# Moving three pieces of VectorE's order, and half of the last stores to a second queue, in a transform-and-ELU kernel

## The chip, the cores and the metric

The kernel runs on one core of a Trainium2 chip. The metric is the device time of one execution in microseconds (us). Every experiment was run several times on one chip together with runs of the kernel before, and is compared with those alone. One execution of each kernel was taken with the hardware profiler; quoted profile lines are from it. Where medians are given they are of all executions of the row.

## The reference

```python
batch, seq, dim = 8, 3008, 256          # x: float32
X = np.fft.fft(np.fft.fft(x, axis=1), axis=2).real
h = X.reshape(24064, 256) @ w_in        # w_in: 256 x 2048
g = np.where(h > 0, h, np.exp(np.minimum(h, 0)) - 1)
out = g @ w_out                         # w_out: 2048 x 256
```

## The kernel before

The transform over the channels is folded into the weights: W1 becomes a cosine part Wc and a sine part Ws. What is left of the transform runs over the sequence, as matrix products with constants (MC); it fills rings from which the tiles read: Rr (real part), Ir (imaginary part), and Rb, one channel's row on all partitions, which E adds with its weights wex. 47 tiles of 256 columns pass over these rings. A tile has eight steps. In each step TensorE (PE) makes

- P, the even sum, H <- Rr,Wc (four matmuls into one bank of PSUM);
- Q, the odd sum, H <- Ir,Ws, written on top of P in the same bank.

VectorE (DVE) has to read P out before Q may start. That copy is E. From E and H (now P + Q) come both signs, P + Q and P - Q, which go through the ELU and into the second product. This product uses a scheme with fewer multiplications and four accumulators pA to pD, which are combined at the end of a tile by DVE. The third of these combinations, comb_22, is what part (a) of the change moves:

```python
def mm_P(i):                             # even sum
    S.H = bank("H");  first_mm(i, Wc, Rr, True)
def mm_Q(i):                             # odd sum, on top of it in the same bank
    first_mm(i, Ws, Ir, False)
def even_part(i):                        # E: has to come between the two
    ...  scalar_tensor_tensor(out=S.E[:, c], in0=Rb[:, cols(i)],
             scalar=wex[:, f : f + 1], in1=S.H[:, c], op0=ALU.mult, op1=ALU.add)

def comb_1(q):  ...  vtt(two(T.u), <T.p1 twice>, two(T.acc[1]), ALU.add)       # u <- p, pB
def comb_2(q):  ...  vtt(two(T.v), <u's half twice>, two(T.acc[2]), ALU.add)   # v <- u, pC
def comb_22(q): vtt(T.u[:, TW:512], T.v[:, TW:512], T.acc[2][:, 0:TW], ALU.add)  # u <- v, pC
def comb_3(q):  vtt(T.v, T.v, T.acc[3], ALU.add)                               # v <- v, pD
def turn_u(q):  ...  nc.vector.transpose(out=T.o[:, 0:512], in_=T.u);  store(...)
def turn_v(q):  ...  nc.vector.transpose(out=T.o[:, 512:1024], in_=T.v);  store(...)
```

The program is a list of (time, action) pairs, `at(t, action)`, sorted by time. The time only decides the order in which an engine gets its instructions; T = 4.8 is the nominal step. The last row of Ir is brought by a small transfer, `Ir[127:128] <- Rb[127:128]`, called Ir<-Rb here. Loads and stores are issued from SyncE's queue (SP).

Folding the 256 channels into pairs for 128 partitions leaves channel 128 over, the "extra channel" that goes into Rb. For the first batch it is made during the start-up. For the others it is fetched as four-byte elements while the first tiles run, transformed in a small product of its own (H <- MC,xe), and spread into the rings.

Three more words are used below. A DFT is a group of the transform's own matmuls (H <- MC,...), set between the steps of some tiles to fill the rings. Folds are sums and differences of input rows that the transform starts from. The fields of a weight chunk are integer work by which DVE prepares a piece of the weights.

Of the kernel before, what the change touches and what calls it, by code (L numbers as in the profile page):

```python
# [77 lines left out]
def kernel(  # L78
# [7 lines left out]
    nc = tc.nc  # L86
# [3 lines left out]
    n_tiles = (n_cols + TW - 1) // TW  # L90
# [796 lines left out]
    def turn_u(q):  # L887
        T = tiles[q]
        T.o = spool.tile([128, 1024], FP, tag="ot", bufs=2, name="ot")
        pin(nc.vector.transpose(out=T.o[:, 0:512], in_=T.u))  # L890
        store(q, 0, 1, 0)
        store(q, 1, 0, 1)

    def turn_v(q):
        T = tiles.pop(q)
        tiles[q, 1] = T
        pin(nc.vector.transpose(out=T.o[:, 512:1024], in_=T.v))
        tiles[q] = T
        store(q, 2, 0, 0)
        store(q, 3, 1, 1)  # L900
        del tiles[q], tiles[q, 1]

    def store(q, part, sg, half):

        T = tiles[q]
        j, end = q * TW, min((q + 1) * TW, n_cols)
        while j < end:
            b, c = divmod(j, HALF)
            odd, cc = divmod(c, RUN)
            i = j - q * TW  # L910
            n = min(end - j, RUN - cc)
            k = 2 * cc + odd
            if sg == 0:
                lo, row, m = i, k, n
            else:
                lo, row = TW - i - n, SEQ - k - 2 * (n - 1)
                m = n - 1 if k == 0 else n
            at_, left = lo, m
            while left:
                p = at_ % 32  # L920
                if p or left < 32:
                    w, nb = min(left, 32 - p), 1
                else:
                    w, nb = 32, left // 32
                r0 = b * SEQ + row + 2 * (at_ - lo)
                for g in range(4):
                    o = part * TW + at_ - p
                    nc.sync.dma_start(
                        out=bass.AP(
                            tensor=out.tensor,  # L930
                            offset=out.offset + r0 * ND + half * 128 + 32 * g,
                            ap=[[2 * ND, w], [64 * ND, nb], [1, 32]],
                        ),
                        in_=T.o[32 * g + p : 32 * g + p + w, o : o + 32 * nb].rearrange(
                            "p (j a) -> p j a", a=32
                        ),
                    )
                at_ += w * nb
                left -= w * nb
            j += n  # L940
# [65 lines left out]
    def fold_now(keys):  # L1006
        for key in keys.split():
            ops[key, 0]()
# [9 lines left out]
    def at(t, fn):  # L1018
        events.append((t, len(events), fn))

    def at_chunk(t, chunk):
        at(t, chunk.fields)
        at(t + 0.01, chunk.power)
        at(t + 0.02, chunk.round)
        at(t + 1.4, chunk.scale)
# [44 lines left out]
    at(-5.8, lambda: state["x_even"].minus())  # L1070
    at(-5.7, lambda: nc.sync.dma_start(out=Ir[127:128, 0:RUN], in_=Rb[127:128, 0:RUN]))
    at_chunk(-5.0, w1_chunks[2])
    at(0.5, lambda: fold_now("EO1 EO3"))
    at(-1.7, w1_chunks[6].load)
    at(-1.6, w1_chunks[7].load)
    at(-1.5, w2_chunks[3].load)
# [3 lines left out]
    T = PERIOD  # L1080
    for chunk, k, second in (
        (w1_chunks[3], 0, 0),
        (w2_chunks[0], 0, 1),
        (w1_chunks[4], 1, 0),
        (w2_chunks[1], 1, 1),
        (w1_chunks[5], 2, 0),
        (w2_chunks[2], 2, 1),
        (w1_chunks[6], 3, 0),
        (w2_chunks[3], 3, 1),
        (w1_chunks[7], 4, 0),  # L1090
        (w2_chunks[4], 4, 1),
        (w2_chunks[5], 5, 1),
        (w2_chunks[6], 6, 1),
        (w2_chunks[7], 7, 1),
    ):
        t = k * T + (1.0 if second else 0.3 if k == 0 else -0.5)
        at(t, chunk.fields)
        at(t + 0.02, chunk.power)
        at(t + 0.05, chunk.round)
        at(k * T + (3.7 if second else 1.7), chunk.scale)  # L1100
    for c in range(1, 8):
        t = (c - 2) * T + 4.7 if c > 1 else 1.0
        at(t, lambda c=c: fold_chunk(c))
        t = (c - 1) * T + 1.4 if c > 1 else 2.0
# [15 lines left out]
    for i in range(total):  # L1120
        t = i * T
# [21 lines left out]
        (1.45, comb_copy),  # L1143
        (4.2, comb_1),
        (4.21, comb_2),
        (4.22, comb_22),
        (T + 2.5, comb_3),
    )
    for q in range(n_tiles):
        t = (8 * q + 9) * T  # L1150
        for dt, fn in (COMB if q else ((1.45, plain_u), (T + 1.1, plain_v))) + (
            (2 * T + 4.2, turn_u),
            (3 * T + 4.2, turn_v),
        ):
            at(t + dt, lambda fn=fn, q=q: fn(q))
# [56 lines left out]
    for n in range(16):  # L1212
        j, k = divmod(n, 4)
# [87 lines left out]
```

## Time and profile before

| | kernel before |
|---|---|
| median of the first three runs | 1999.42 us |
| span of the profiled run | 1997.2 us |
| PE busy | 1969.3 us |
| PE waiting for E | 13.4 us in 15 waits |
| PE's last row starts | 1984.83 us |
| from there to the end of the span | 12.4 us |

The last line is the difference of the two numbers above it and the span. The page also shows the span in 40 slices of some 50 us, each digit a busy share in tenths:

```profile
PE   8899999999999999999999999999999999999997
...
DVE  7866656666666655676566665666566665566665
...
DMA  8228100121001110011100211003010110000101
```

PE is at nine tenths or more nearly everywhere. Only the first two slices and the last are lower, and the DMA engines are at eight tenths only in the first. So the kernel is bound by PE; what can be won lies in a start-up of some 100 us, in the last slice, and in gaps between matmuls too small for this picture. The prediction shows those gaps.

### The profile page before, as it was taken

What the parts mean: (1) busy time and instruction counts of PE and PEld (TensorE: products, weight loads), DVE (VectorE), ACT (ScalarE), POOL (GpSimd) and SP (SyncE); (2) the same over time, 40 slices, a digit from 0 to 9 for tenths busy, and PEclk for the clock granted to TensorE, in tenths of its full rate; (3) what the DMA queues carried; (4) which work ended last, traced back from release to release, by engine and by line L of the source; (5) the groups of instructions that cost most, each with busy time, mean ns of one, the idle gap of its engine ahead of it and who ended that gap; (6) DMA issues with size and microseconds to landing.
All of it is one profiled execution on the core that took longest, in us unless ns stands there. A gap on an engine that the chain in (4) does not pass through costs nothing.

```text
span 1997.2 us, 26765 instructions
## 1 busy us (share of the span) xinstructions
PE 1969.3 (99%) x8895; PEld 1662.1 (83%) x8896; DVE 1284.2 (64%) x2342; ACT 861.0 (43%) x1651; POOL 1334.0 (67%) x1820
## 2 busy tenths in 40 slices
PE   8899999999999999999999999999999999999997
PEld 5788888888888888888888888888888888888886
DVE  7866656666666655676566665666566665566665
ACT  2544444443444434444444443444434443444443
POOL 2578757786577755777567775678657776555664
PEclk9999999999999999999999999999999999999999
DMA  8228100121001110011100211003010110000101
GB/s 320 85 20 63 47 15 16 38 59 21 16 20 43 45 29 11 18 43 46 26 18 12 66 24 26 11 19 89 7 19 12 22 19 15 15 12 13 20 12 22
DMA packets 256044, 71.61 MB, mean 36 GB/s; under 512 B 244303, under 2 KB 245092, under 8 KB 255394
## 3 DMA queue, kind: packets, MB, share of 16 engines
q1 hardware_dynamic: 253506, 57.32, 14.6%
q0 software_dynamic: 2400, 12.59, 1.9%
q8 instruction: 70, 1.15, 0.2%
q14 instruction: 68, 0.56, 0.1%
HBM read 45.02 MB, written 24.80 MB: 35 GB/s over the span
## 4 chain that ended last, share of the span: by engine, by line
PE 93%; DVE 4%; ACT 1%; issue 1%; DMA 1%; POOL 1%; DVEq 0%; ACTq 0%; POOLq 0%; SPq 0%
PE H L353 37%; PE pB L353 16%; PE pD L353 15%; PE pC L353 15%; PE pA L353 8%; DVE E L715 1%; PE M L353 1%; DVE G L741 1%; DVE u L359 0%; DVE v L359 0%; DVE G L725 0%; POOL G L362 0%; DMA xl<-in_x_dram 0%; ACT G L365 0%; DVE w L220 0%
## 5 line engine op out<-in xcount | busy, mean ns | idle before, releaser
L362 POOL TENSOR_TENSOR G<-G 128x256 f32<-128x256 f32 x1472 | 1057.6, 728 | 588.3 <-DVE G L741 474.7
L715 DVE SCALAR_TENSOR_TENSOR E<-Rb,wex,H 128x256 f32<-128x256 f32 x752 | 327.6, 477 | 616.3 <-PE H L353 615.7
L365 ACT ACTIVATE G<-H 128x512 f32<-128x512 f32 x376 | 224.5, 597 | 955.3 <-DVE G L725 955.3
L353 PE MATMUL H<-Ir,Ws 128*128 128x256 f32 x1504 | 392.4, 383 | 13.4 <-DVE E L715 13.4
L353 PE MATMUL H<-Rr,Wc 128*128 128x256 f32 x1504 | 386.4, 379 | 0.0
L353 PE MATMUL pC<-G,WT 128*128 128x256 f32 x1472 | 377.8, 379 | 0.0
L353 PEld LDWEIGHTS H<-Ir,Ws 128*128 128x128 f32 x1504 | 276.3, 190 | 72.5 <-DVE E L715 28.8
L353 PEld LDWEIGHTS H<-Rr,Wc 128*128 128x128 f32 x1504 | 285.1, 190 | 53.2 <-issue 2.5
L353 PEld LDWEIGHTS pC<-G,WT 128*128 128x128 f32 x1472 | 279.7, 190 | 38.0
L725 DVE SCALAR_TENSOR_TENSOR G<-E,H 128x512 f32<-128x512 f32 x376 | 257.0, 684 | 37.9 <-issue 0.9
L741 DVE SCALAR_TENSOR_TENSOR G<-G,H 128x512 f32<-128x512 f32 x376 | 255.6, 680 | 31.7 <-ACT G L365 31.6
L741 DVE SCALAR_TENSOR_TENSOR G<-M,G 128x512 f32<-128x512 f32 x376 | 256.6, 683 | 0.0
L353 PE MATMUL pB<-G,w 128*128 128x256 f32 x800 | 234.8, 380 | 0.0
L353 PE MATMUL pA<-G,w 128*128 128x256 f32 x800 | 234.1, 379 | 0.5 <-issue 0.5
L365 ACT ACTIVATE G<-G 128x512 f32<-128x512 f32 x376 | 233.3, 620 | 0.0
L365 ACT ACTIVATE M<-G 128x512 f32<-128x512 f32 x376 | 224.1, 596 | 0.0
L365 ACT ACTIVATE M<-M 128x512 f32<-128x512 f32 x376 | 221.0, 588 | 0.1
L353 PE MATMUL pB<-G,WT 128*128 128x256 f32 x736 | 219.2, 379 | 0.5 <-POOL G L362 0.5
L353 PE MATMUL pD<-G,WT 128*128 128x256 f32 x736 | 219.1, 379 | 0.6 <-DVE v L359 0.4
L353 PE MATMUL pD<-G,w 128*128 128x256 f32 x736 | 218.9, 379 | 0.0
L353 PEld LDWEIGHTS pB<-G,w 128*128 128x128 f32 x800 | 152.7, 191 | 21.0
L353 PEld LDWEIGHTS pA<-G,w 128*128 128x128 f32 x800 | 151.9, 190 | 21.5 <-POOL w L362 0.9
(136 smaller groups left out, 1337.2 us busy)
## 6 DMA issues: line engine op xcount, KB each, us to landing
out_dram<-ot SPq DMA_DIRECT2D x504, 32.0 KB
xl<-in_x_dram SPq DMA_DIRECT2D x16, 768.0 KB
MC<-dft_mats SPq DMA_DIRECT2D x4, 1131.0 KB
out_dram<-ot SPq DMA_DIRECT2D x256, 2.0 KB
Rb<-r SPq DMA_DIRECT2D x10, 376.0 KB
raw<-in_moe_w_in_dram SPq DMA_DIRECT2D x6, 512.0 KB
raw<-in_moe_w_out_dram SPq DMA_DIRECT2D x6, 512.0 KB
out_dram<-ot SPq DMA_DIRECT2D x64, 28.0 KB
```

What stands on the lines that cost most here:

```text
L353: nc.tensor.matmul(out_, lhsT=lhsT, rhs=rhs, start=start, stop=stop, skip_group_check=True)
L362: pin(nc.gpsimd.tensor_tensor(out=o, in0=a, in1=b, op=op))
L365: pin(nc.scalar.activation(out=o, in_=i, func=func, **kw))
L715: nc.vector.scalar_tensor_tensor(out=S.E[:, c], in0=Rb[:, cols(i)], scalar=wex[:, f : f + 1], in1=S.H[:, c], op0=ALU.mult, op1=ALU.add,)
L725: nc.vector.scalar_tensor_tensor(out=two(S.G[:, 0:512])[:, :, ::-1], in0=two(S.E), scalar=2.0, in1=two(S.H), op0=ALU.mult, op1=ALU.subtract,)
L741: nc.vector.scalar_tensor_tensor(out=o, in0=e, scalar=-1.0, in1=h, op0=ALU.add, op1=ALU.max)
```

## The change

Five edits, in three parts. (a) The third combination (comb_22) moves behind the next step's E at each tile boundary, so that E, for which PE waits, no longer stands behind it. (b) In step 0, E goes ahead of the fields of a weight chunk and of two folds in DVE's order. (c) In the last tile u's transpose comes before the last sum, and every second of the last 16 stores is issued from ScalarE's queue.

```diff
-                    nc.sync.dma_start(
+                    queue = nc.scalar if q == n_tiles - 1 and g % 2 else nc.sync
+                    queue.dma_start(
 ...
-    at(0.5, lambda: fold_now("EO1 EO3"))
+    at(1.3, lambda: fold_now("EO1"))
+    at(3.9, lambda: fold_now("EO3"))
 ...
-        t = k * T + (1.0 if second else 0.3 if k == 0 else -0.5)
+        t = k * T + (1.9 if second and k == 0 else 1.0 if second or k == 0 else -0.5)
 ...
-        (4.22, comb_22),
+        (T + 1.0, comb_22),
 ...
-            (2 * T + 4.2, turn_u),
+            (2 * T + 4.2 if q < n_tiles - 1 else T + 2.4, turn_u),
```

## The prediction

> **What bounds the kernel now.** I read the page first, then who TensorE (PE) waited for, then the timeline at three places: a tile boundary, step 0 and the end.
>
> ```profile
> PE 1969.3 (99%) x8895; PEld 1662.1 (83%) x8896; DVE 1284.2 (64%) x2342; ACT 861.0 (43%) x1651; POOL 1334.0 (67%) x1820
> ```
>
> PE is busy for 1969.3 of 1997.2 us. The change removes no matmul, so its whole field is the 28 us in which PE does nothing, plus stalls that hide inside PE's rows. The view of PE's waits:
>
> ```profile
> PE H L353 <- DVE E L715: 13.4, 15, 4.7
> PE M L353 <- DVE zero L340: 1.1, 1, 1.1
> PE pA L353 <- issue: 0.5, 1, 0.5
> PE pB L353 <- POOL G L362: 0.5, 1, 0.5
> PE pD L353 <- DVE v L359: 0.4, 2, 0.2
> ```
>
> Nearly all waiting (columns: total us, times, longest) is the second half of a step's first matmul group (Q: H from Ir and Ws, which writes on top of the even sum in H) waiting until VectorE (DVE) has read the even sum out (E, L715). The same view cut at 120 us gives 10.7 us in 6 waits before it and 2.7 us in 9 waits after it. The other idle time of PE is the tail: its last matmul starts at 1984.83 and runs 0.59, so some 11.8 us of the span come after it.
>
> A boundary between two tiles, from the timeline (start, duration):
>
> ```profile
> 727.09 0.69 DVE L359 TENSOR_TENSOR v<-u,pC 128x512 f32<-128x512 f32 x1
> 727.81 0.42 DVE L359 TENSOR_TENSOR u<-v,pC 128x256 f32<-128x256 f32 x1
> 728.15 0.87 DVE L715 SCALAR_TENSOR_TENSOR E<-Rb,wex,H 128x256 f32<-128x256 f32 x2
> 728.17 0.59 PE L353 MATMUL pB<-G,WT 128*128 128x256 f32 x2
> 729.07 1.13 PE L353 MATMUL H<-Ir,Ws 128*128 128x256 f32 x4 [0.30 <-DVE E L715]
> 729.53 0.68 DVE L359 TENSOR_TENSOR v<-v,pD 128x512 f32<-128x512 f32 x1
> ```
>
> DVE runs without a gap, and the third combination (u<-v,pC) delays E by 0.34 us (727.81 to 728.15). Q starts 0.90 us after the pB row in front of it; in an undisturbed step the same distance is 0.43 (1961.71 to 1962.14).
>
> Step 0 and the end:
>
> ```profile
> 28.51 0.62 SPq L1071 DMA_DIRECT2D Ir<-Rb  x1
> 30.96 1.89 PE L353 MATMUL H<-w,CC 128*128 128x256 f32 x8
> 33.73 0.94 DVE L426 TENSOR_TENSOR e<-e,e 128x768 f32<-128x768 f32 x1
> 34.60 2.05 DVE L426 TENSOR_TENSOR o<-o,o 128x762 f32<-128x762 f32 x1
> 36.57 0.86 DVE L715 SCALAR_TENSOR_TENSOR E<-Rb,wex,H 128x256 f32<-128x256 f32 x2
> 37.50 2.06 PE L353 MATMUL H<-Ir,Ws 128*128 128x256 f32 x4 [4.65 <-DVE E L715]
> ...
> 1985.84 0.69 DVE L359 TENSOR_TENSOR v<-v,pD 128x512 f32<-128x512 f32 x1
> 1986.45 0.70 DVE L890 STREAM_TRANSPOSE ot<-u 128x512 f32<-128x512 f32 x1
> 1987.08 0.67 DVE L897 STREAM_TRANSPOSE ot<-v 128x512 f32<-128x512 f32 x1
> 1987.18 7.71 SPq L928 DMA_DIRECT2D out_dram<-ot  x16
> ```
>
> In step 0, E stands in DVE's order behind a chunk's fields and both folds, so PE sits for 4.65 us and then runs slow (the clock windows read 0.50 from 36.6 to 43.3). At the end one queue issues 16 stores in 7.71 us, 0.48 each, back to back, while the DMA engines are 0.41 busy and move 66 GB/s, which is 32 KB per 0.48 us: the issue sets that pace.
>
> **What the Trainium skill says.** "TensorE: Matmul & The Clock Gate", Part 1: the clock halves after an idle window of about 3.4 us and returns after a busy one; windows run freely. The trace agrees roughly: it fell at 36.6, 3.7 us after PE stopped, and was back at 43.4; but it also fell at 77.5 after a wait of 2.34 us, so a window need not be wholly idle. "DMA: Bandwidth & Descriptors", Issuing engines are not separate DMA queues: several issuing engines save only the sequencer's time to initiate. At the end that time is the bound. Same page, Queues, rings and completion order: on each DMA engine descriptors are consumed in ring order. This matters for Ir<-Rb below.
>
> **The change part by part.** Comparing the two programs engine by engine, PE's order is the same. On DVE the third combination moves behind E at every tile boundary; step 0's E moves ahead of the chunk's fields and the folds; in the last tile u's transpose comes before the last sum. Eight of the last 16 stores go to ScalarE's queue.
>
> (a) *Third combination.* I went through all but the last of the boundaries in the timeline, 45 of them. At 37, Q starts 0.05 to 0.06 us after E's end, so E holds it; the view lists only the longer waits. At 28 of these 37 the distance from the row before is 0.52 instead of 0.43, and the row after Q comes 0.97 after it instead of 0.87 (a stalled Q restarts cold): 0.09 + 0.10 = 0.19 us lost. A tile without a DFT shows the same: its boundaries lie 38.18 us apart (325.14 to 363.32), while eight undisturbed steps (1964.73 to 1969.48, 4.75 each) make 38.0. At the other 9 the distance is 0.85 to 1.01. With E 0.34 earlier the 28 lose nothing more, and the 9 gain about 0.34 each: 28 x 0.19 + 9 x 0.34 = 5.3 + 3.1 = 8.4 us gained, all on PE, so on the path. Against it: at the other 8 boundaries, where a DFT's matmuls sit before the step, E waits for PE, and the combination now filling DVE's idle time will come after E and push the last sum (v<-v,pD) by 0.34. pD is written next; its slack behind that sum is 0.75 us at five of the 8 and 0.14 (nothing) at three (972, 1018, 1420). Those three should wait 0.34 more: 1.0 us lost. Net gain: 7.4 us. pC itself is rewritten 0.9 us after Q starts, and the combination ends about 0.35 us after E, so no wait there.
>
> (b) *Step 0.* If E alone held Q, E would start at 32.06 when Ir's sums end, and Q could start near 33, at the end of the fold's matmuls. But Q also reads the row that Ir<-Rb brings, and that transfer was issued at 28.5 behind two matrices of 1131 KB on a queue that runs full at 390 GB/s until about 40.2. Adding up the bytes moved against the issue order, the first of these two should have left the queue at 32.3; the next issue that needed its slot stopped waiting at about 34.2, 1.9 us later. The second ends by the same sum at 35.0, so Ir<-Rb would land near 37 (estimate: 35.0 + 1.9), and the trace only says that it was there by 37.5. Then Q gains 0.4 to 1 us and the clock still falls. If it lands before 36, PE keeps its clock and gains some 4 us by step 1, when DVE's queue (both folds, fields, rounding in front of the next E) and the chain from Ws through DRAM to wex take over. I weigh these about 2 to 1: 1.6 us gained.
>
> (c) *Last tile.* u's transpose starts at 1985.84 instead of 1986.45, so the first store goes out 0.61 us earlier. v's transpose ends near 1987.85, before u's eight stores are issued on two queues (4 x 0.48 = 1.9 us from 1986.57). The last issue then ends at 1986.57 + 8 x 0.48 = 1990.4 instead of 1994.9: 4.5 us. The 2.3 us from there to the end stay. The DMA engines would be 0.82 busy, which leaves room but little; a store also waits for the landing of the one eight before it, which comes twice as soon. I take 3.9.
>
> Sum: 7.4 + 1.6 + 3.9 = 12.9 us, and 1999.4 - 12.9 = 1986.5.
>
> **The rivals.** *Step 0 only trades waits* (the DMA of Ir takes E's place): the byte count speaks for it; against it, only the chance that a small transfer lands ahead of the slowest engine's share. With the other parts whole, 1999.4 - 7.4 - 4.5 - 0.4 = 1987.1; if it is wrong and the clock holds, 1983.5. *The stores are bound below the issue* (descriptor generation shared, or writes of 128 bytes that get slower together): the even 66 GB/s would look the same in this case. Then (c) gains 0.6 and the total is 1999.4 - 7.4 - 1.6 - 0.6 = 1989.8. *The boundary gives the time back*: DVE has no gap there, so moving 0.34 us inside its order could move the wait to pD or to the sums on GpSimd. Slack of 0.69 us at pD speaks against it, as does the fact that g_plus ends where it did before. If half of (a) came back: 1990.2. *A cold first transfer on ScalarE's queue* could cost about 1 us of (c): 1987.5.
>
> **Range and chances.** (a) rests on many equal boundaries, 5.5 to 8.4; (b) spans 0.2 to 4.7; (c) 0.6 to 4.7. They don't hang together, so the extremes rarely meet: 1983.0 to 1990.3. 2% is 40 us, more than all of PE's idle time, so a large gain is out; a loss of that size would need a wait repeated at every tile that the order of instructions doesn't show.
>
> **What would show it.** (a): after 120 us the waits for E nearly vanish, tiles without a DFT take 38.0 us instead of 38.18, and pD waits for v near 975, 1021 and 1424. (b): Q of step 0 starts near 37 with E done by 33; if it starts by 34 I misjudged the transfer. (c): two queues with eight issues each in about 4 us, 120 GB/s or more, and 4 to 4.5 us less after PE's last matmul. I'd be wrong if the tail stays at 66 GB/s, or if the tile period doesn't change.

## The result, and the profile after

| | before | changed |
|---|---|---|
| median | 1999.41 us (4 runs) | 1987.13 us (4 runs) |
| all runs | 1998.81 to 1999.43 | 1984.7, 1985.63, 1988.63, 1992.6 |
| span of the profiled run | 1997.2 us | 1982.9 us |

The ratio is 0.9943 (95% interval 0.9921 to 0.9965), so "within 2%". A ratio here is the mean time of one kernel's fast runs over the mean of the other's of the same rounds, so not quite the ratio of the medians; in the experiments below the profiled execution, which came first, is in the median but not in the ratio. The medians differ by 12.3 us, against 12.9 predicted. Note that the profiled run of the changed kernel (1984.7) was its fastest, so differences between the two traces are a little too kind to it.

The whole view of PE's waits after the change (total us, times, longest):

```profile
PE H L353 <- DVE E L715: 6.6, 6, 2.2
PE H L353 <- DMA Ir<-Rb: 4.7, 1, 4.7
PE pD L353 <- DVE v L359: 1.5, 3, 0.5
PE M L353 <- DVE zero L340: 1.1, 1, 1.1
PE pA L353 <- issue: 0.5, 1, 0.5
PE pB L353 <- POOL G L362: 0.5, 1, 0.5
```

The waits for E fell from 15 to 6, and all six lie before 120 us. But a wait of 4.7 us, as long as the longest for E had been, now stands at Ir<-Rb, and pD waits three times for the last sum.

The same tile boundary as in the prediction, from the timeline (start, duration, engine, operation):

```profile
723.06 0.69 DVE L359 TENSOR_TENSOR v<-u,pC 128x512 f32<-128x512 f32 x1
...
723.66 0.87 DVE L715 SCALAR_TENSOR_TENSOR E<-Rb,wex,H 128x256 f32<-128x256 f32 x2
...
724.14 0.59 PE L353 MATMUL pB<-G,WT 128*128 128x256 f32 x2
...
724.45 0.41 DVE L359 TENSOR_TENSOR u<-v,pC 128x256 f32<-128x256 f32 x1
...
724.58 1.13 PE L353 MATMUL H<-Ir,Ws 128*128 128x256 f32 x4
```

Q now starts 0.44 us after the pB row in front of it (724.14 to 724.58), not 0.90. Before, E started 1.06 us after v<-u,pC (727.09 to 728.15); now it is 0.60 (723.06 to 723.66). So taking the combination out of the way was worth 0.46 us, although only 0.34 lay between its start and E's. The other 0.12 us stand in front of it: v<-u,pC to u<-v,pC, which reads its result, took 0.72 us before, while v<-u,pC to the independent E takes 0.60 now.

One of the three boundaries where the prediction expected a loss, in the kernel before and then in the changed one:

```profile
977.41 0.67 PE L353 MATMUL pD<-G,WT 128*128 128x256 f32 x2 [0.20 <-DVE v L359]
```

```profile
972.25 0.67 PE L353 MATMUL pD<-G,WT 128*128 128x256 f32 x2 [0.54 <-DVE v L359]
```

The bracket says that PE idled until v, the last sum, was done. It happens at 972.25, 1018.53 and 1418.49, each time 0.33 to 0.34 us longer than before: 0.54, 0.47 and 0.54 us instead of 0.20, 0.14 and 0.20. The view of waits leaves out the one of 0.14 and so shows 0.4 us before; by the starts of the rows it was 0.55, and it is 1.55 now.

Step 0:

```profile
28.50 0.62 SPq L1072 DMA_DIRECT2D Ir<-Rb  x1
...
31.97 0.86 DVE L715 SCALAR_TENSOR_TENSOR E<-Rb,wex,H 128x256 f32<-128x256 f32 x2
...
37.84 2.04 PE L353 MATMUL H<-Ir,Ws 128*128 128x256 f32 x4 [4.67 <-DMA Ir<-Rb]
```

E was done near 32.8, some 5 us before Q. Yet Q began at 37.84, later than the 37.50 of before, because Ir<-Rb, issued at 28.50, kept it.

The end:

```profile
1974.77 0.59 PE L353 MATMUL pD<-G,w 128*128 128x256 f32 x2
1975.26 0.42 DVE L359 TENSOR_TENSOR u<-v,pC 128x256 f32<-128x256 f32 x1
1975.71 0.71 DVE L890 STREAM_TRANSPOSE ot<-u 128x512 f32<-128x512 f32 x1
1976.35 0.65 DVE L359 TENSOR_TENSOR v<-v,pD 128x512 f32<-128x512 f32 x1
1976.45 3.83 SPq L929 DMA_DIRECT2D out_dram<-ot  x8
1976.46 3.95 ACTq L929 DMA_DIRECT2D out_dram<-ot  x8
```

Two queues issue eight stores each, side by side, in 3.95 us where one needed 7.71 for sixteen. From 1978 to 1981 us the core moves 130 GB/s; before, from 1988 to 1994, it moved 67. From PE's last row to the end it is now 8.1 us (1982.9 - 1974.77).

So the two traces differ by 14.3 us of span. The tail gives 12.4 - 8.1 = 4.2 of them (from unrounded ends). The start of the thirteenth Q, near 126 us, moved from 126.80 to 125.11: 1.7. What remains, 8.4, is in the tile boundaries.

### The profile page after: what moved, and what is told of

Same layout as the page of the kernel before. It is cut to its first block, busy times and chain, and to the rows that moved or that the text cites. A ratio compares the mean times of both kernels' runs of the same rounds, so it can differ in the third digit from the quotient of the medians.

```text
span 1982.9 us, 26811 instructions
## 1 busy us (share of the span) xinstructions
PE 1960.3 (99%) x8896; PEld 1661.3 (84%) x8896; DVE 1280.8 (65%) x2342; ACT 861.0 (43%) x1651; POOL 1333.5 (67%) x1820
## 3 DMA queue, kind: packets, MB, share of 16 engines
q0 software_dynamic: 2400, 12.59, 1.9%
## 4 chain that ended last, share of the span: by engine, by line
PE 94%; DVE 3%; DMA 1%; ACT 1%; issue 0%; POOL 0%; DVEq 0%; POOLq 0%; ACTq 0%; SPq 0%
PE H L353 38%; PE pB L353 16%; PE pD L353 16%; PE pC L353 16%; PE pA L353 8%; DVE E L715 0%; DMA Ir<-Rb 0%; DMA xl<-in_x_dram,ix 0%; DVE o L426 0%; DVE G L741 0%; DMA wex<-wx 0%; DVE e L426 0%; DMA wx<-Ws 0%; DVE v L359 0%; ACT w L365 0%
## 5 line engine op out<-in xcount | busy, mean ns | idle before, releaser
L353 PE MATMUL H<-Ir,Ws 128*128 128x256 f32 x1504 | 388.6, 381 | 11.3 <-DVE E L715 6.6
```

Source lines behind the costliest of these rows:

```text
L353: nc.tensor.matmul(out_, lhsT=lhsT, rhs=rhs, start=start, stop=stop, skip_group_check=True)
```

## The experiments

Eleven runs of nine kernels were made, on three chips (after_again and after_third are the changed kernel, lx_ir_again is after_lx_ir once more). All gave correct results. "Before" is the median of 11 runs of the kernel before on the same chip.

| run | chip | median us | before | ratio (95% interval) |
|---|---|---|---|---|
| a_only | 1 | 1990.5 | 1998.29 | 0.9959 (0.9946 to 0.9971) |
| b_only | 1 | 1998.85 | 1998.29 | 1.0011 (0.9998 to 1.0024) |
| c_only | 1 | 1994.21 | 1998.29 | 0.9979 (0.9966 to 0.9992) |
| after_again | 1 | 1987.09 | 1998.29 | 0.995 (0.9936 to 0.9963) |
| c_queue | 2 | 1995.28 | 1998.91 | 0.9989 (0.9969 to 1.0008) |
| before_ir | 2 | 1998.66 | 1998.91 | 1.0003 (0.9982 to 1.0024) |
| after_lx | 2 | 1986.65 | 1998.91 | 0.9935 (0.9923 to 0.9946) |
| after_lx_ir | 2 | 1983.6 | 1998.91 | 0.992 (0.9907 to 0.9934) |
| after_third | 3 | 1985.9 | 1999.58 | 0.9925 (0.9901 to 0.995) |
| lx_ir_again | 3 | 1983.63 | 1999.58 | 0.9909 (0.9886 to 0.9932) |
| best | 3 | 1982.46 | 1999.58 | 0.9904 (0.9881 to 0.9927) |

### The parts alone

The theory was the prediction's sum of three independent parts; the rival, that the parts overlap or that one of them earns all.

**a_only**: the kernel before with one edit.

```diff
-        (4.22, comb_22),
+        (T + 1.0, comb_22),
```

> Only the third combination behind E. The parts-add-up theory: PE loses nothing more at 28 boundaries (0.19 us each) and 0.34 us less at 9, and waits 0.34 us more at three: 7.4 us predicted; the changed kernel's trace gave 8.4 us between 126.8 us and the last matmul, so 1991.0 to 1992.0 us, and runs as close together as before's (0.1 us). Rival (DVE gives it back elsewhere): 1995 us or more. If the changed kernel's wide spread (1984.7 to 1992.6) comes from this part, these runs spread over several us.

Measured: 7.8 us under the kernel before (1998.29 - 1990.5). After 120 us the view of PE's waits has no line for E any more:

```profile
PE H L353 <- POOL xe L362: 6.9, 1, 6.9
PE pD L353 <- DVE v L359: 1.5, 3, 0.5
PE pB L353 <- POOL G L362: 0.5, 1, 0.5
```

The three waits of pD are there, and at the boundaries this trace shows what the changed kernel's shows: 5.3 us gained at 28 of them, 4.1 at 9, 1.0 lost at 3. The first line belongs to the profiled execution alone, which took 2001.16 us while the other five took 1989.2 to 1990.76; it is taken up below.

**b_only**: the kernel before with the two edits of step 0 (the fold and the chunk times of the diff above).

> Only step 0's order. Theory (the row brought by Ir<-Rb bounds the second half of step 0, not E): Q of step 0 still starts between 37 and 38 us, the wait is put down to the DMA, and the gain is 0 to 2 us: 1997.5 to 1999.5. Rival (E was the bound): Q near 33 us and 1995 us. The spread of the changed kernel should lie here, since its wait now ends with a transfer: runs several us apart. Rival for the spread: these runs lie within 0.1 us and it comes from the stores on two queues or from the combination.

Measured: 0.6 us above the kernel before, with an interval that reaches to no difference at all. From its timeline:

```profile
37.85 1.10 PE L353 MATMUL H<-Ir,Ws 128*128 128x256 f32 x4 [3.92 <-DMA Ir<-Rb]
```

E ended near 34.4 in this run. Q started at 37.85 all the same.

**c_only**: the kernel before with the second queue and the early transpose.

> Only the last tile. Theory (the issue of one queue set the pace): 16 stores issued in 3.9 us on two queues, tail 4.2 us shorter: 1995.2 us, spread 0.1 us. Rival (the two queues share what generates descriptors): issue rows near 0.9 us each and 1998.8 us. Rival for the spread: runs several us apart.

Measured: 4.1 us under the kernel before.

**after_again**: the changed kernel, on the same chip.

> The changed kernel once more, for its spread and a second trace. Theory: median 1986 to 1988, runs spread over 4 to 8 us again, and the traces differ only in the first 100 us (landing of Ir<-Rb, clock windows, wait at the fifth step). Rival: the spread is of one bad run or chip and is gone: all within 0.5 us.

Measured: 11.2 us under the kernel before. The three parts alone sum to 7.8 - 0.6 + 4.1 = 11.3. So they add up within what the medians can tell, and (b) adds nothing that shows. The expectation that the two traces of the changed kernel differ only in the first 100 us was wrong: this one waits 4.27 us near 194 us (see below).

### The second queue without the early transpose

**c_queue**: the kernel before with the queue's edit alone.

```diff
-                    nc.sync.dma_start(
+                    queue = nc.scalar if q == n_tiles - 1 and g % 2 else nc.sync
+                    queue.dma_start(
```

> The kernel before with only the last tile's stores on two queues, the transpose left behind the last sum. Theory: the two queues are worth 3.6 us (7.7 to 3.9 us of issue, less the wait for v's transpose), the order 0.6 us: 1994.7. Rival (the early transpose is what counts): about 1997.5.

Measured: 3.6 us by the medians; the interval of the ratio reaches to no difference, because one execution took 2001.72 us. The trace is sharper, since it can be read from PE's last row:

```profile
1983.32 0.59 PE L353 MATMUL pD<-G,w 128*128 128x256 f32 x2
...
1985.67 3.84 SPq L929 DMA_DIRECT2D out_dram<-ot  x8
1985.68 3.96 ACTq L929 DMA_DIRECT2D out_dram<-ot  x8
```

The span ended at 1992.1, that is 8.8 us after 1983.32. The kernel before needed 12.4, c_only and the changed kernel 8.1. So the queue gives 3.6 us and the early transpose 0.7.

### Why the early E gained nothing in step 0

Theory: Q needs two things, E and the row of Ir<-Rb. Both came at nearly the same time before, and only one was moved. Rival: PE waits for something else that neither edit touches.

**before_ir**: the kernel before, with the transfer alone moved to ScalarE's queue.

```diff
-    at(-5.7, lambda: nc.sync.dma_start(out=Ir[127:128, 0:RUN], ...))
+    at(-5.7, lambda: nc.scalar.dma_start(out=Ir[127:128, 0:RUN], ...))
```

> The kernel before with only Ir<-Rb on ScalarE's queue. Theory (there E, behind the fields and folds, held Q): within 0.5 us of before, Q of step 0 at 37 to 37.8 us as before. Rival (the transfer was the true bound in before too and only the put-down of the wait was wrong): 3 us faster.

Measured: no gain (1998.66 against 1998.91). Its step 0 waits for E, as in the kernel before:

```profile
37.63 2.07 PE L353 MATMUL H<-Ir,Ws 128*128 128x256 f32 x4 [4.81 <-DVE E L715]
```

And c_queue, which has the kernel before's order in step 0, names the other cause in its own execution:

```profile
37.70 2.05 PE L353 MATMUL H<-Ir,Ws 128*128 128x256 f32 x4 [4.61 <-DMA Ir<-Rb]
```

There E ended near 37.5, and the transfer was still later. Two conditions arrived within some tenths of a microsecond of each other; which one came last differed between executions of the same order.

**after_lx_ir** does both: E early and the transfer on ScalarE's queue. It also carries the later extra channel described in the next part; the run to compare it with is after_lx on the same chip.

> The same, with Ir<-Rb issued on ScalarE's queue instead of behind the two matrices on SyncE's. Theory (the ring's order held the row back): it lands within 3 us, Q of step 0 starts near 33.2 us with no wait over 0.5 us, the clock doesn't fall there, the next wait is of the odd transform for EO1 (about 1.5 us) and the gain over after_lx is 3 to 4.5 us: 1982 to 1983.5. Rival (the DMA engines are simply full): lands near 37 us again and 0 to 0.5 us gained.

Measured: 1983.6 against 1986.65 us, a gain of 3.05 us that neither change has alone.

```profile
28.46 0.60 ACTq L1072 DMA_DIRECT2D Ir<-Rb  x1
...
32.25 0.87 DVE L715 SCALAR_TENSOR_TENSOR E<-Rb,wex,H 128x256 f32<-128x256 f32 x2
...
33.81 1.10 PE L353 MATMUL H<-Ir,Ws 128*128 128x256 f32 x4 [1.47 <-DMA Ir<-Rb]
...
44.20 0.87 DVE L715 SCALAR_TENSOR_TENSOR E<-Rb,wex,H 128x256 f32<-128x256 f32 x2 [0.89 <-DMA wex<-wx]
...
45.12 2.07 PE L353 MATMUL H<-Ir,Ws 128*128 128x256 f32 x4 [3.26 <-DVE E L715]
```

The same transfer, issued at the same time, released Q after 5.4 us instead of 9.3. That is so in the two other runs with this edit as well (5.38 in both, one of them issued 1 us later), while in the six traces that wait for it on SyncE's queue Q starts between 37.43 and 37.85 whether it was issued at 28.32 or at 30.04: there its place in the queue set the time. The expectation, within 3 us, was too short all the same. The skill's "DMA: Bandwidth & Descriptors", Queues, rings and completion order, says that each DMA engine takes turns, packet by packet, between the queues that have work for it. That fits: on ScalarE's queue the transfer need not let the matrices ahead of it on SyncE's queue finish. The runs show the gain; the turns themselves they don't show. Q runs at full clock here (1.10 us, not 2.04). Not all of the 4 us survive: the next E now waits for the chain of wx and wex through DRAM, and PE for 3.26 us behind it, which is the limit that the prediction had named.

### The executions that are longer than the others

In the first rounds the changed kernel's times spread over 8 us. In the profiled executions of a_only and after_again (2001.16 and 1991.25 us, each well above its median) PE waits for the extra channel. First the kernel before, then after_again, from the timeline:

```profile
191.40 2.09 PE L353 MATMUL H<-MC,xe 128*8 128x377 f32 x24
```

```profile
194.16 4.01 PE L353 MATMUL H<-MC,xe 128*8 128x377 f32 x24 [4.27 <-POOL xe L362]
```

(In a_only the wait is 6.9 us, and the product after it takes 4.18 us, not 2.09.) The four-byte loads of that channel run slower in these executions. Five of them, one after the other on the queue, in the kernel before and in a_only:

```profile
154.78 10.67 SPq L565 DMA_DIRECT2D x<-in_x_dram  x5
```

```profile
155.39 13.89 SPq L565 DMA_DIRECT2D x<-in_x_dram  x5
```

Theory: the program gives these loads too little room, and where they are slow PE stops, whatever the change. Rival: the change's own new order makes the spread.

**after_lx**: the changed kernel with all work on the extra channel that follows its loads six steps later, and its spreading into one batch's ring seven steps later.

```diff
-    at(24.4 * T, get_ext)
-    at(25 * T + 1.35, fold_ext)
-    at(25 * T + 4.75, dft_ext)
+    at(30.4 * T, get_ext)
+    at(31 * T + 1.35, fold_ext)
+    at(31 * T + 4.75, dft_ext)
 ...  (five more lines, each 6 * T later)
-            step = s0 + (28, 38)[kodd]
+            step = s0 + (35 if b == 1 else 28, 38)[kodd]
```

> The changed kernel with the extra channel's transform (waits for xe) moved six steps later; its result is first read after step 40. Theory (the wide spread is PE waiting for xe in executions in which the 4-byte loads run slowly): all runs within about 1.5 us of each other, median 1985.5 to 1987, no wait of PE for POOL xe. Rival (the spread comes from step 0's transfer, the clock or the stores): single runs still 4 us or more above the others.

Measured: six executions between 1986.03 and 1987.56 us, and no wait for xe. The median is that of the changed kernel; what went is the spread. A later run of this placement shows it more directly. In lx_ir_again (the run is told of in the next part) the loads were slow too:

```profile
149.72 12.59 SPq L565 DMA_DIRECT2D x<-in_x_dram  x5
```

Yet PE did not wait for xe, and this execution, 1983.61 us, lies among the five others. Of the nine profiled executions with the old placement, the two with slow loads (12.89 and 13.89 us) are the two in which PE waits; in the other seven the five loads take 10.67 to 10.79. Over all rounds, the four runs with this edit made 23 executions, none over 1.8 us above the fastest of its row, while the changed kernel made 16, of which four (1991.25, 1991.85, 1992.6, 1995.26) lie 4 us or more above its medians. The kernel before has such executions too (five of 37 lie between 2004 and 2009 us). So have b_only (2002.04, 2006.72), before_ir (2005.51) and c_queue (2001.72), so the new order is not what makes them. That they come from the same loads is likely but not shown: none of them was profiled. Why the loads are slow at times stays open.

### A version that beats both

The three waits of pD are a price of moving the third combination at boundaries where E waits for PE in any case. **best** is after_lx_ir with the old place kept there:

```diff
+    dft_steps = {HALF * 8 // TW * b + s for b in range(NB - 1)
+                 for s in (28, 30, 34, 36, 38, 40, 42, 44)}
 ...
+        comb = tuple((4.22 if fn is comb_22 and 8 * q + 9 in dft_steps else dt, fn)
+                     for dt, fn in COMB)
```

> The changed kernel with three additions: the transfer Ir<-Rb on ScalarE's queue, the work on the extra channels six steps later (both as in the run before), and the third combination kept in front of the even part at the eight boundaries where a DFT's matmuls stand before the step, so that there the even part waits for TensorE anyway and the combination costs nothing in front of it. Theory: in the changed kernel the last sum of three of these boundaries came 0.34 us late and TensorE waited 1.5 us in all for it (the view of waits: pD for v, 1.5, 3, 0.5); with the old order there these three waits go and nothing else appears, so about 1.0 to 1.5 us below the same kernel without this part, near 1982.5 us. Rival: the three stalls also let other work catch up, or the even part at these boundaries is not as late as I read it; then waits for E of some 0.3 us come back at up to eight places, and the time is the same as without it or up to 1.5 us longer.

> The changed kernel with the transfer Ir<-Rb on ScalarE's queue and the extra channels' work six steps later, once more, to be compared with its neighbours on the same chip. Expected: 1983.6 us again within 1 us, the wait of step 0 for Ir<-Rb under 2 us, full clock there, no execution lengthened by a wait for the extra channels, and three waits of pD for v, 1.5 us in all. Rival: the 3 us were the other chip's or a favourable order of transfers in that run, and the gain over the changed kernel is under 2 us here.

> The changed kernel for a third time, as the measure for the two others on this chip. Expected: median 1987 us, 11 to 12.5 us under the kernel before, and again one or two executions that are 3 to 8 us longer, because TensorE waits for the extra channels when their four-byte loads take longer than 12 us per five. Rival: those outliers belong to single chips; then all executions here lie within 2 us.

Measured on one chip: best 1982.46, lx_ir_again 1983.63, after_third 1985.9 us. The whole view of PE's waits after 120 us in best:

```profile
PE pB L353 <- DVE u L359: 0.5, 1, 0.5
PE pD L353 <- DVE v L359: 0.4, 2, 0.2
PE H L353 <- DVE E L715: 0.3, 1, 0.3
```

pD waits 0.4 us in this view, as in the kernel before, and lx_ir_again has 1.6 in three waits. With the short wait that the view leaves out the difference is 1.0 us (1.56 against 0.57 by the starts of the rows); the medians differ by 1.17. The rival, that waits for E come back at these boundaries, fell: the one of 0.3 us stands in lx_ir_again too. The gain of lx_ir_again over after_third, 2.3 us, is less than the 3.05 of the other chip but over the 2 us that the rival was given. after_third again had one longer execution in six (1991.85). The long executions of the kernel before on this chip (four of 11) lift its median, so the difference of the medians, 13.7 us for after_third, is too kind. By its median best is 0.17% under the changed kernel, and its ratio to the kernel before is 0.9904 where the changed kernel has 0.9925.

## Why the prediction was right or wrong

**The total was right** (1986.5 predicted, 1987.13 measured, range 1983.0 to 1990.3), and so was the class. That it came so close is in part luck: by the traces (a) was 1.0 us too small, (c) 0.3 too small and (b) 1.6 too large, and these errors cancel.

**(a) Right, with one term too small.** The mechanism held. In the changed kernel none of the 28 boundaries for which 0.19 us was predicted has the longer distances left: 0.43 or 0.44 before Q and 0.86 or 0.87 after it. A tile without a DFT takes 37.98 us (323.51 to 361.49) where it took 38.18. The three losses came at the three places named, 1.0 us in all (1.55 against 0.55), as predicted. The term that was mis-sized is "the 9 gain about 0.34 each". They gained 0.45 each on average: besides the 0.34, the 0.12 us by which the third combination starts later behind v<-u,pC than E does now. 28 x 0.19 + 9 x 0.45 = 5.3 + 4.1 = 9.4; less 1.0 that is 8.4. This is just what the traces show between the start-up and the tail. They could have gained a little more: at seven of the nine Q still starts 0.05 us after E's end, and the row after it still comes 0.97 us later, not 0.87. The medians of a_only give 7.8.

**(b) Wrong.** The prediction gave 1.6 us, weighing two outcomes. The likelier of them happened, "Step 0 only trades waits", with Q at 37.84 where the estimate had Ir<-Rb near 37. But even that outcome was sized at 0.4 to 1 us, and it gave nothing. The step that failed is the estimate that "Ir<-Rb would land near 37": in the traces that wait for it on SyncE's queue Q is released between 37.43 and 37.85 (37.84 in the changed kernel), no earlier than the 37.50 at which E released it before. The landing before 36, to which one chance in three was given, came in no trace on that queue. The 1.7 us by which the start-up differs between the two first traces is not a gain: with the old order the thirteenth Q begins at 126.80, 127.59, 125.93, 125.17 and 126.91 in five traces, with the new one at 125.11, 126.01, 125.41, 126.79 and 127.00. The means are 126.5 and 126.1 and the spread is 2 us. With the transfer moved as well it is 123.25, 123.34 and 124.61. A part of that spread is the clock: the first trace of the kernel before has half clock from 36.6 to 43.4, that of the changed kernel only from 37.2 to 40.7, after waits of 4.65 and 4.67 us.

**(c) Right.** 3.9 us were predicted and 4.1 (c_only) to 4.2 (trace) measured. By the trace's own terms: the issue is 7.71 - 3.95 = 3.8 us shorter; the first store comes 1.68 us after PE's last row (1974.77 to 1976.45) instead of 2.35 (1984.83 to 1987.18), 0.7 us; and from the last issue to the end it is 2.5 us instead of 2.3, 0.2 us lost. The rival of a limit below the issue fell: sixteen stores go out in half the time, at 130 GB/s instead of 67. So did the one of a cold first transfer on ScalarE's queue.

**Not foreseen:** the single executions 3 to 11 us above the median, which is as much as a part of the change gives. The range was not made for them: it holds the median, but not the execution of 1992.6 us.

## What to carry to other kernels

Before removing a wait, list everything that the waiting instruction needs, and compare their arrival times: a profile names only the last, and when two come within tenths of a microsecond, as E and Ir<-Rb did, moving one earns nothing, moving both earned 3 us. A short instruction in front of the one that others wait for can cost more than its own time (here 0.46 us, not 0.34), so measure from the instruction before it. A small transfer that something waits for does not belong behind large ones on the same queue, and stores at the very end are worth two queues when the trace shows the issue back to back.

## What the Trainium skill lacked or had wrong

- "TensorE: Matmul & The Clock Gate", Part 1: that windows run freely, so that one kernel sees different ramps, is right (half clock for 6.8 us in one trace and 3.4 in the other, after waits of the same length). Its table gives at least one idle window of about 3.4 us as the condition; in the kernel before the clock also fell, at 77.6 us, after a wait of only 2.34 us.
- "DMA: Bandwidth & Descriptors", Issuing engines are not separate DMA queues: the time saved by a second issuing engine is called usually small relative to the DMA itself. Here it was 3.8 us of a tail of 12.4, with sixteen stores of 32 KB.
- The same page, Queues, rings and completion order: it has no figure for how long a small transfer waits behind large ones. Here the same transfer released its reader after 9.3 us behind two matrices of 1131 KB (7.8 where it was issued 1.5 us later), and after 5.4 us on the other queue.
- No page that was read gives the extra cost on VectorE of an instruction that reads the result of the one just before it: 0.72 us from start to start, against 0.60 with an independent one behind the same instruction (that the reading is the reason was not tested apart).
- No page that was read says that loads of four-byte elements differ between executions of one program: 10.67 us for five in one, 12.59, 12.89 and 13.89 in others.
